# Pooled V from a second read of V, pooled keys as two halves of 72: an attention-then-MLP kernel on one core

## The chip, the core and the metric

The kernel runs on one core of a Trainium2 chip. The time is the device time of one execution in microseconds (us); the median of three runs before the change is 328.3 us (327.95 to 328.8). The core has a matmul engine, TensorE (PE in the profile; its weight loads are listed apart as PEld), three engines for elementwise work (VectorE or DVE, ScalarE or ACT, GpSimd or POOL), a queue engine (SyncE or SP) that issues transfers, and 16 DMA engines that carry them. Data lies in SBUF, 128 partitions wide; matmuls write to PSUM, which GpSimd is not used to read here.

## What is computed

Two parts in a row. Attention over 8 batches, 8 heads, 576 tokens, head size 64, done twice and added:

```python
q_d = q.reshape(B, H, Sd, 4, D).mean(axis=3)      # k_d and v_d in the same way; Sd = 144
out_up = np.repeat(sm_attn(q_d, k_d, v_d), 4, axis=2)
mask = np.abs(pos[:, None] - pos[None, :]) < 4     # local: three tokens to each side
out_local = softmax(where(mask, scale * q @ k.T, -1e9)) @ v
x = (out_up + out_local)  # to rows of 512 = 8 heads x 64, 4608 tokens
h = x @ w_in              # 512 -> 2048
out = (h - tanh(h)) @ w_out   # 2048 -> 512
```

## The kernel before

**Pairs.** Attention goes by pairs of heads: pair p of 32 is batch p // 4, heads 2j and 2j + 1 with j = p % 4. `attention(p)` casts q and k (L452, `qr`), transposes them, from pair 8 on by a DMA transpose (`qT`, L457), puts them in order (`qk`, L465), and pools q and k by sums of four tokens in two additions (`half`, L499; `qkd`, L508). The local scores are five tiles of 128 keys against 112 or 120 queries (`score`, L517). The pooled scores (L539) use `qkd`, whose 144 positions are kept as five overlapping groups of 32, GW = 160 columns, so that pooled positions follow the five tiles of queries; the keys are taken as two overlapping sets of 128. Exponentials are taken on ACT (L557, L569, L572) into `E`, and a 0/1 mask is multiplied in, the big one on DVE (L561), the small one (tile 4, 240 columns, L576) on DVE or GpSimd. Then the values: ten matmuls against `vw` (L585) and eight against the pooled `vd` (L591); a 65th column of ones, or of 0 and 4, gives the sums for the division (L602, L604). The result goes back through a DMA transpose (`lT`, L621) and a `join` of local and pooled parts into `xT` (L633, L637).

**V.** `load_v` brings V as five overlapping tiles of 128 tokens (`vst`, L357), `prep_v` casts it (`vw`, L390). Once for two pairs `pool_v` forms pooled V with TensorE: four matmuls with 32 columns of weights (L405) and one with 128 (L407) into a PSUM bank that the scores or the values use too, copied to `vd` by ACT (L412).

**Dense work.** When a batch's four pairs are in `xT`, `dense` adds its matmuls: `mm1` (L675), tanh on ACT (L686), the difference on DVE (L689), `mm2` (L711), a copy (L726) and the store (L730).

**Order.** `Program` collects all operations with a cost in ns, their reads and writes and a priority, and `order` plays them through engine by engine with these costs; what it gives is the order of instructions of every engine, fixed when the program is built. A `choice` goes to the engine that is free first. Dense matmuls have the last priority, so they fill what attention leaves. SyncE issues in this order: loads of pair p wait, from pair 12 on, until `lT` of pair p - 5 has been issued (`GATE`, `BEHIND`). `SMALL` is the first pair whose small mask may go to GpSimd. Buffers: `vd` and `vw` three, `qk`, `qkd`, `E` two, `vst` five, `qkn` four.

Of the kernel before, what the change touches and what calls it, by code (L numbers as in the profile page):

```python
# [165 lines left out]
def kernel(  # L166
# [21 lines left out]
    NT = 5  # L188
    GS = KW // 4
    PIECES = [(0, 0, 120), (1, 0, 112), (2, 0, 56), (2, 56, 56), (3, 0, 112), (4, 0, 120)]  # L190
    GW = 32 * NT
# [227 lines left out]
    def attention(p):  # L419
# [8 lines left out]
        biased = p < BIASED  # L428

# [72 lines left out]
        def add2(eng):  # L502
            with nc.allow_low_precision("pooled q and k"):
                out = qkd[s].rearrange("p i (t r) -> p i t r", t=NT)
                a, c = (bass.AP(tensor=half.tensor, offset=half.offset + e,
                                ap=[half.ap[0], [2 * G, 2], [2 * GS, NT], [2, 32]])
                        for e in range(2))
                eng.tensor_tensor(out=out, in0=a, in1=c, op=ALU.add)  # L508
# [20 lines left out]
        def s2(bank=ps):  # L529
# [6 lines left out]
            for i in range(2):  # L536
                for hh in range(2):
                    rows = slice(64 * hh, 64 * hh + 64)
                    T.matmul(bank[:, hh, 120 + GW * i:120 + GW * i + GW],  # L539
                             qkd[s][rows, 1, 32 * i:32 * i + 128],  # L540
                             qkd[s][rows, 0], start=True, stop=True)
# [14 lines left out]
        e3 = E[s][:, 1152:1792].rearrange("p (h c) -> p h c", h=2)  # L556
# [9 lines left out]
        if not merged:  # L566
# [6 lines left out]
            out=e3, in_=ps2[:, :, 120:120 + 2 * GW], func=AF.Exp, scale=SCALE / 16.0),  # L573
# [7 lines left out]
        def outs():  # L581
            for hh in range(2):
# [4 lines left out]
                for half in range(2):  # L587
                    c = 1152 + 2 * GW * hh + 128 * half
                    o = 65 * (NT + half)
                    for i in range(2):  # L590
                        T.matmul(po[:, hh, o:o + 65],  # L591
                                 E[s][:, c + GW * i:c + GW * i + 128],
                                 vd[w][:, i, 2 * jj + hh, :],
                                 start=(i == 0), stop=(i == 1))
        if p == 2:
# [3 lines left out]
           reads=[("E", s, 0), ("E", s, 1), ("E", s, 2), ("vw", w, jj), ("vd", w)],  # L599
# [20 lines left out]
        if XOUT[p] == 'dma':  # L620
# [7 lines left out]
            def join(eng):  # L628
# [3 lines left out]
                          for a, n, m in ((x, 456, 120), (pool, 130, 30)))  # L632
# [7 lines left out]
                    in1=pool[:, 32:128].rearrange("p (t g) -> p t g", t=3)[:, :, 2:30]  # L640
# [125 lines left out]
    BYACT = 0  # L766
    T_IN, T_OUT = 1550, 1200
    NOACT = 0
    SMALL = 12
# [131 lines left out]
```

## Time and profile before

| what | value |
|---|---|
| runs, median (lowest to highest) | 328.3 us (327.95 to 328.8) |
| the profiled execution's own time, its span | 327.29 us, 325.6 us |
| granted TensorE clock | 1.0 |
| busy: PE, DVE, ACT, POOL | 313.9, 212.5, 224.7, 165.6 us |
| DMA | 109715 packets, 59.79 MB |
| values of pair 16, 28 and 31 begin (L585, with L602 for the last) | 132.0, 224.6, about 245 us |

Lines beginning with L are groups of instructions: line, engine, operation, output and inputs, shape, count, then busy us and mean ns of one, then the engine's idle time just before them and what ended it. Lines that begin with a number are the timeline: start, length, engine, line, and in brackets the idle time before. "A:B" lines are stretches of the span with the busy time of each engine. Lines with three times and slashes give the minimum, median and maximum of a group in ns. Matmul rows are longer than their slots, since successive matmuls overlap.

### The profile page before, as it was taken

To read this page: it belongs to the slowest core of one execution; us is meant where nothing else is said; L and a number is where in the kernel's file an instruction comes from. 1 tells how busy PE (TensorE), PEld (TensorE's weight loads), DVE (VectorE), ACT (ScalarE), POOL (GpSimd) and SP (SyncE) were. 2 spreads that over 40 slices of the span, in tenths; PEclk is the share of its full clock that TensorE was granted. 3 is DMA by queue.
4 is the path that set the end of the run, shared out by engine and by line. 5 is a ranking of instruction groups with operands and counts; after the bars stand their busy time and mean duration, and the time that the engine had idled before them with its cause. 6 is when DMAs were issued, how large, how long until landed. Compare 5 with 4: busy or idle time off the path is not lost.

```text
span 325.6 us, 7167 instructions
## 1 busy us (share of the span) xinstructions
PE 313.9 (96%) x2643; PEld 175.5 (54%) x2686; DVE 212.5 (65%) x388; ACT 224.7 (69%) x390; POOL 165.6 (51%) x230
## 2 busy tenths in 40 slices
PE   6899999999899999999999999999999999999996
PEld 2565555666544445666654444656554445566544
DVE  6898985789966576765867576778665444554311
ACT  3765987599888969799986978798973444544300
POOL 5688758265846767677767767877440000000000
PEclk9999999999999999999999999999999999999999
DMA  7999999899987999699999999995322001000022
GB/s 205 316 393 367 372 315 273 216 259 217 240 254 106 254 201 294 92 234 219 191 233 165 261 209 263 222 229 106 85 66 62 32 32 67 32 34 32 32 84 81
DMA packets 109715, 59.79 MB, mean 184 GB/s; under 512 B 92656, under 2 KB 92912, under 8 KB 109680
## 3 DMA queue, kind: packets, MB, share of 16 engines
q1 hardware_dynamic: 109680, 59.33, 72.9%
q8 instruction: 21, 0.34, 0.5%
q14 instruction: 14, 0.11, 0.1%
HBM read 37.75 MB, written 9.44 MB: 145 GB/s over the span
## 4 chain that ended last, share of the span: by engine, by line
PE 90%; DVE 4%; issue 2%; POOL 1%; DMA 1%; ACT 1%; SPq 0%; POOLq 0%
PE ps_hy L711 38%; PE ps_hy L675 36%; PE ps_ox L517 3%; PE ps_ox L585 3%; PE ps_ox L591 2%; PE ps_ox L539 1%; PE ps_ox L405 1%; PE ps_ox L618 1%; PE ps_ox L407 1%; DVE ln L604 1%; DVE gT L689 1%; DMA qkn<-in_k_dram 1%; PE ps_ox L615 1%; PE ps_ox L482 1%; PE ps_ts L482 1%
## 5 line engine op out<-in xcount | busy, mean ns | idle before, releaser
L675 PE MATMUL ps_hy<-xT,w_in_sb 128*128 128x320 bf16 (+1 forms) x759 | 146.9, 325 | 1.7 <-DVE gT L689 1.0
L711 PE MATMUL ps_hy<-w_out_sb,gT 128*128 128x512 bf16 (+1 forms) x559 | 139.0, 373 | 2.2 <-issue 1.0
L689 DVE TENSOR_TENSOR gT<-ps_hy,u 128x320 bf16<-128x320 f32 (+1 forms) x192 | 103.2, 553 | 56.0 <-ACT u L686 53.1
L686 ACT ACTIVATE u<-ps_hy 128x320 f32<-128x320 f32 (+1 forms) x192 | 93.6, 497 | 53.2 <-PE ps_hy L675 47.3
L675 PEld LDWEIGHTS <-w_in_sb 128*128 128x128 bf16 x768 | 71.8, 98 | 53.4 <-issue 1.7
L711 PEld LDWEIGHTS <-gT 128*128 128x128 bf16 x592 | 56.0, 98 | 52.8
L499 POOL TENSOR_TENSOR half<-qk 128x576 f32<-128x576 bf16 x29 | 33.3, 1148 | 48.7 <-ACT qk L465 33.9
L465 ACT COPY qk<-qT 128x576 bf16<-128x576 bf16 x44 | 52.3, 1207 | 0.0
L452 POOL CAST qr<-qkn 128x576 bf16<-128x576 f32 x48 | 33.4, 707 | 13.0 <-DMA qkn<-in_k_dram 6.2
L604 DVE TENSOR_TENSOR ln<-ps_ox,r 128x896 bf16<-128x896 f32 x32 | 34.9, 1091 | 1.1
L561 DVE TENSOR_TENSOR E<-E,mask 128x912 bf16<-128x912 bf16 x28 | 24.0, 856 | 10.4 <-ACT E L557 10.4
L557 ACT ACTIVATE E<-ps_ox 128x912 bf16<-128x912 f32 x28 | 26.2, 937 | 4.9 <-PE ps_ox L517 4.6
L726 DVE COPY y<-ps_hy 128x512 f32<-128x512 f32 (+1 forms) x21 | 13.9, 663 | 20.2 <-PE ps_hy L711 19.1
L390 POOL CAST vw<-vst 128x640 bf16<-128x640 f32 x32 | 25.5, 796 | 2.4 <-DMA vst<-in_v_dram 2.3
L508 POOL TENSOR_TENSOR qkd<-half 128x320 bf16<-128x320 f32 x29 | 23.9, 823 | 1.8 <-DVE r L602 1.1
L572 ACT ACTIVATE E<-ps_ox 128x640 bf16<-128x640 f32 x28 | 20.0, 716 | 0.0
L585 PE MATMUL ps_ox<-vw,E 128*128 128x65 bf16 x320 | 19.3, 194 | 0.4 <-ACT vd L412 0.3
L585 PEld LDWEIGHTS <-E 128*128 128x128 bf16 x320 | 16.4, 98 | 5.7 <-issue 0.3
L576 POOL TENSOR_TENSOR E<-E,mask 128x240 bf16<-128x240 bf16 x18 | 13.6, 756 | 9.4 <-ACT E L569 9.3
L591 PE MATMUL ps_ox<-vd,E 128*128 128x65 bf16 x256 | 18.0, 193 | 0.1
L517 PEld LDWEIGHTS <-qk 64*128 64x128 bf16 x320 | 9.2, 95 | 16.1 <-issue 12.5
L602 DVE RECIPROCAL r<-ps_ox 128x14 f32<-128x14 f32 x32 | 7.7, 242 | 14.3 <-PE ps_ox L591 12.4
(78 smaller groups left out, 240.2 us busy)
## 6 DMA issues: line engine op xcount, KB each, us to landing
vst<-in_v_dram SPq DMA_DIRECT2D x64, 160.0 KB, 4.2
qkn<-in_q_dram SPq DMA_DIRECT2D x32, 288.0 KB, 4.1
qkn<-in_k_dram SPq DMA_DIRECT2D x32, 288.0 KB, 4.1
out_dram<-y SPq DMA_DIRECT2D x35, 256.0 KB, 2.5
gT<-in_moe_w_in_dram SPq DMA_DIRECT2D x4, 1024.0 KB, 8.1
xT<-in_moe_w_out_dram SPq DMA_DIRECT2D x8, 256.0 KB, 5.2
gT<-in_moe_w_out_dram SPq DMA_DIRECT2D x2, 1024.0 KB, 10.2
qT<-qr SPq DMA_TRANSPOSE x24, 4.2
```

The lines of the kernel that those rows point to most:

```text
L390: P.choice([(eng, ns, lambda fn=fn: fn(out=vw[w][:, 2 * jj:2 * jj + 2, :, 0:64], in_=vst[s])) for eng, ns, fn in CAST_V[p >= NEARLY]], rea ...
L452: P.choice([(eng, ns, lambda dst=dst, srt=srt, fn=fn: fn(out=dst, in_=srt)) for eng, ns, fn in (any3[2:] if p >= CASTS else any3[:1] + any ...
L465: fn(out=full[:, i].rearrange("p (g a) -> p g a", a=A9), in_=qT[s][:, :, i::2].rearrange("p a g -> p g a"))
L499: eng.tensor_tensor(out=half, in0=four[:, :, :, 0:2], in1=four[:, :, :, 2:4], op=ALU.add)
L557: op("ACT", 820, lambda: A.activation(out=e1, in_=ps[:, :, 0:456], func=AF.Exp, scale=SCALE), reads=ts, writes=[("E", s, 0)], pri=pri)
L585: T.matmul(po[:, hh, 65 * t:65 * t + 65], E[s][:, c:c + 128], vw[w][:, 2 * jj + hh, t, :], start=True, stop=True)
L591: T.matmul(po[:, hh, o:o + 65], E[s][:, c + GW * i:c + GW * i + 128], vd[w][:, i, 2 * jj + hh, :], start=(i == 0), stop=(i == 1))
L604: op("DVE", 1010, lambda: V.tensor_tensor(out=ln[s].rearrange("p n (h d) -> p h n d", d=D), in0=blocks[:, :, :, 0:64], in1=r[s].unsqueeze( ...
L675: T.matmul(ps_hy[slot][:, 0:n], w_in_sb[:, dc, fc * 128:(fc + 1) * 128], xT[dc][:, t0 + c0:t0 + c0 + n], start=(dc == 0), stop=(dc == N_DC ...
L686: op("ACT", 90 + 76 * n // 100, lambda: A.activation(out=u[us][:, 0:n], in_=ps_hy[slot][:, 0:n], func=AF.Tanh), reads=[("hy", slot)], writ ...
L689: op("DVE", 70 + 105 * n // 100, lambda: V.tensor_tensor(out=gT[g][:, fc, c0:c0 + n], in0=ps_hy[slot][:, 0:n], in1=u[us][:, 0:n], op=ALU.s ...
L711: T.matmul(ps_hy[slot][:, 0:c1 - c0], gT[g][:, fc, ts * 128:ts * 128 + 128], w_out_sb[:, fc, c0:c1], start=(fc == 0), stop=(fc == N_FF - 1))
```

## The change

From pair 16 on (`DIRECT`) pooled V no longer comes from `pool_v`, which returns at once. `load_pool` reads V of each head once more, in rows of four tokens: 72 partitions, two rows of 256 numbers on each, into the space of batches 0 and 1 of `xT` (two buffers for each head). These 32 transfers stand in SyncE's queue and, as the other loads, behind the `lT` of five pairs earlier; for pairs 16 and 17 also behind the dense matmuls that read this space. `sum_v` adds the four tokens on GpSimd in two additions for each head and writes `vd` as two sets of 72 keys. For these pairs the pooled positions are plain: `qkd` has 144 columns, the pooled scores are 72 x 144 twice for each head, the exponential takes 72 partitions, and the pooled value matmuls contract 72 rows. `SMALL` becomes 8.

```diff
-    GW = 32 * NT
+    GW, KP = 32 * NT, G // 2
+    def load_pool(p):
+        b, j, n = p // NP, p % NP, p % 2
+        for i in range(2):
+            def issue(i=i, base=v[b, 2 * j + i]):
+                nc.sync.dma_start(out=vp(n, i), in_=bass.AP(
+                    tensor=base.tensor, offset=base.offset,
+                    ap=[[4 * D, KP], [KP * 4 * D, 2], [1, 4 * D]]))
+            load(650, issue, [("vp", n, i)] + [("x", c, 2 * n + i) for c in (0, 1)] * (p < DIRECT + 2),
+                 T_P, -30 + 0.06 + 0.1 * p, behind=[("sent", p - BEHIND)])
+    def vp(n, i):
+        t = xT[2 * n + i][0:KP, 0:1024].bitcast(FP32)
+        return t.rearrange("p (e x) -> p e x", e=2)
+    def sum_v(p):
+        n, w, jj = p % 2, (p // 2) % NVW, p % 2
+        if p < DIRECT + 2 * NVW:
+            op("DVE", 70, lambda: V.memset(vd[w][0:KP, jj, :, 64:65], 4.0),
+               writes=[("vd", w)], pri=10 * p - 12)
+        for i in range(2):
+            t = vp(n, i)
+            def add1(eng, t=t):
+                eng.tensor_tensor(out=t[:, :, 0:128], in0=t[:, :, 0:128],
+                                  in1=t[:, :, 128:256], op=ALU.add)
+            def add2(eng, t=t, i=i):
+                with nc.allow_low_precision("pooled v"):
+                    eng.tensor_tensor(out=vd[w][0:KP, jj, 2 * i:2 * i + 2, 0:64],
+                                      in0=t[:, :, 0:64], in1=t[:, :, 64:128], op=ALU.add)
+            for n1, fn in ((330, add1), (220, add2)):
+                P.choice([("POOL", n1, lambda fn=fn: fn(GP))],
+                         reads=[("vp", n, i)] + [("vd", w)] * (p < DIRECT + 2 * NVW),
+                         writes=[("vp", n, i)] if fn is add1 else [("vdd", w, jj, i)],
+                         pri=10 * p - 8)
     def pool_v(hb):
+        if 2 * hb >= DIRECT:
+            return
     def attention(p):
+        direct = p >= DIRECT
+        gw, kp = (G, KP) if direct else (GW, 128)
         def add2(eng):
+                if direct:
+                    eng.tensor_tensor(out=qkd[s][:, :, 0:G], in0=half[:, :, :, 0],
+                                      in1=half[:, :, :, 1], op=ALU.add)
+                    return
-                    T.matmul(bank[:, hh, 120 + GW * i:120 + GW * i + GW],
-                             qkd[s][rows, 1, 32 * i:32 * i + 128],
-                             qkd[s][rows, 0], start=True, stop=True)
+                    k0 = (KP if direct else 32) * i
+                    T.matmul(bank[0:kp, hh, 120 + gw * i:120 + gw * i + gw],
+                             qkd[s][rows, 1, k0:k0 + kp],
+                             qkd[s][rows, 0, 0:gw], start=True, stop=True)
-            out=e3, in_=ps2[:, :, 120:120 + 2 * GW], func=AF.Exp, scale=SCALE / 16.0),
+            out=e3, in_=ps2[0:kp, :, 120:120 + 2 * gw], func=AF.Exp, scale=SCALE / 16.0),
                         T.matmul(po[:, hh, o:o + 65],
-                                 E[s][:, c + GW * i:c + GW * i + 128],
+                                 E[s][0:kp, c + gw * i:c + gw * i + 128],
+                                 vd[w][0:kp, jj, 2 * hh + i, :] if direct else
                                  vd[w][:, i, 2 * jj + hh, :],
...
+    DIRECT, T_P = 16, 430
-    SMALL = 12
+    SMALL = 8
         if nl[0] < NPAIR:
             load_qk(nl[0])
             load_v(nl[0])
+            if nl[0] >= DIRECT:
+                load_pool(nl[0])
...
         if p + 2 < NPAIR:
             prep_v(p + 2)
+            if p + 2 >= DIRECT:
+                sum_v(p + 2)
```

The `join` reads the pooled part at the plain positions for these pairs; the number and shape of its instructions stay.

More of the change, by code (lines that the diff above doesn't have):

```diff
@@ L555, in attention @@
         e2v = E[s][:, 912:1152].rearrange("p (h c) -> p h c", h=2)
-        e3 = E[s][:, 1152:1792].rearrange("p (h c) -> p h c", h=2)
+        e3 = E[s][0:kp, 1152:1152 + 4 * gw].rearrange("p (h c) -> p h c", h=2)
         op("ACT", 820, lambda: A.activation(
@@ L587, in outs @@
                 for half in range(2):
-                    c = 1152 + 2 * GW * hh + 128 * half
+                    c = 1152 + 2 * gw * hh + 128 * half
                     o = 65 * (NT + half)
@@ L598, in attention @@
         op("PE", 590 * cold, outs,
-           reads=[("E", s, 0), ("E", s, 1), ("E", s, 2), ("vw", w, jj), ("vd", w)],
+           reads=[("E", s, 0), ("E", s, 1), ("E", s, 2), ("vw", w, jj), ("vd", w)] +
+           [("vdd", w, jj, i) for i in range(2)] * direct,
            writes=ox, pri=pri)
@@ L631, in join @@
                                   ap=[a.ap[0], [n, 2], [1, m]])
-                          for a, n, m in ((x, 456, 120), (pool, 130, 30)))
+                          for a, n, m in ((x, 456, 120), (pool, 114 if direct else 130, 30)))
                 eng.tensor_tensor(
@@ L639, in join @@
                     in0=lT[s][:, 1:4, 0:112].rearrange("p t (g a) -> p t g a", a=4),
-                    in1=pool[:, 32:128].rearrange("p (t g) -> p t g", t=3)[:, :, 2:30]
+                    in1=(pool[:, 30:114].rearrange("p (t g) -> p t g", t=3) if direct else
+                         pool[:, 32:128].rearrange("p (t g) -> p t g", t=3)[:, :, 2:30])
                     .unsqueeze(3).to_broadcast([128, 3, 28, 4]), op=ALU.add)
```

## The prediction

> **What bounds the kernel now.** I read the page first, for the engine that sets the end; then the stretches of time; then, inside one stretch, single instructions.
>
> ```profile
> PE 313.9 (96%) x2643; PEld 175.5 (54%) x2686; DVE 212.5 (65%) x388; ACT 224.7 (69%) x390; POOL 165.6 (51%) x230
> ...
> PE 90%; DVE 4%; issue 2%; POOL 1%; DMA 1%; ACT 1%; SPq 0%; POOLq 0%
> ```
>
> TensorE is busy for 96% of the span and is 90% of the chain that ended last. A matmul's row is longer than its slot, so I look at one stretch in the middle: from the value matmuls of pair 16 to those of pair 28.
>
> ```profile
> 132.00:224.60 92.60, 91.50 (x823) 51.96 (x836) 64.84 (x112) 78.58 (x132) 68.49 (x91) 1.00 1.02 213
> 246.00:326.00 80.00, 76.09 (x410) 40.69 (x416) 33.05 (x60) 27.44 (x55) 0.00 (x0) 1.00 0.14 50
> ```
>
> The columns are PE, PEld, DVE, ACT and POOL busy, the granted clock (1.00 throughout), the DMA share and GB/s. In the stretch PE idles 1.1 us in 92.6. GpSimd (POOL) is 74% busy, the DMA engines are occupied without a break (1.02). In the last 80 us GpSimd does nothing and the DMA engines little: what is left is dense work on TensorE. So a microsecond of matmul taken away is a microsecond gained, as long as nothing else makes TensorE wait in the attention stretch; and attention has room to end later, since dense matmuls can be moved ahead of it.
>
> **The matmuls removed.** `pool_v` is skipped eight times, once for every two pairs from pair 16 on; each has 4 matmuls with 32 columns of weights and one with 128.
>
> ```profile
> 137.61 1.03 PE L711 MATMUL ps_hy<-w_out_sb,gT 128*128 128x512 bf16 x4
> 138.56 0.29 PE L405 MATMUL ps_ox<-vw,pick 128*32 128x256 bf16 x4
> 138.79 0.29 PE L407 MATMUL ps_ox<-vw,pick 128*128 128x256 bf16 x1
> 138.91 1.25 PE L675 MATMUL ps_hy<-xT,w_in_sb 128*128 128x320 bf16 x8
> ...
> 140.00 0.32 PE L585 MATMUL ps_ox<-vw,E 128*128 128x65 bf16 x5
> ```
>
> Eight L675 take 1.09 us from start to start, 0.136 each with 320 columns; by columns, 512 take 0.218. The four L711 end their slots at 137.61 + 4 x 0.218 = 138.48, and the next dense matmul starts at 138.91. One `pool_v` costs 0.43 us with its switch between tile shapes. Eight make 3.4 us off TensorE's path.
>
> **Pooled scores, 160 queries become 144.**
>
> ```profile
> 135.41 0.30 PE L539 MATMUL ps_ox<-qkd 64*128 64x160 bf16 x4
> 135.65 1.04 PE L711 MATMUL ps_hy<-w_out_sb,gT 128*128 128x512 bf16 x4
> L539 PEld LDWEIGHTS <-qkd 64*128 64x128 bf16 x128 | 4.8, 94 | 0.0
> L405 PEld LDWEIGHTS <-pick 128*32 128x32 bf16 x64 | 1.6, 92 | 4.6 <-ACT u L686 2.0 <-issue 1.3 <-ACT E L569 0.4
> ```
>
> Four matmuls use 0.24 us; a tenth fewer columns is at most 0.024 us for each of 16 pairs, and I take 0.2 us as the gain after what the switch keeps. Their weights go from 128 columns to 72. No row shows a 72-column load. The nearest rows, 128 and 32 columns, differ by 2 ns, so I take no change; the upper bound is that a narrower load costs its whole slot again, 0.06 us x 64 = 3.8 us. The Trainium skill, "TensorE: Matmul & The Clock Gate", Weight-path perf modes, says that the fast weight load is on only when the number of weights is 128, and its LDWEIGHTS section gives P/1.2 ns for P columns, 60 ns for 72 (estimate): by that rule the 64 loads would take 3.8 us in all, and where they are not covered the gain of the whole change would be about eaten. No run here shows it, and 32 columns would be as quick by that formula as by the row.
>
> The value matmuls keep their number and their 65 columns, but the pooled ones contract 72 rows and not 128.
>
> ```profile
> L618 PE MATMUL ps_ox<-up,ln 32*128 32x120 bf16 x10 | 2.2, 222 | 0.0
> L618 PE MATMUL ps_ox<-up,ln 128*128 128x120 bf16 x10 | 2.2, 217 | 0.0
> ```
>
> With 32 rows a matmul took 222 ns, with 128 rows 217: I take nothing, between -0.6 and +0.6 us (128 x 5 ns).
>
> **ACT and DVE** lose eight pooled-value casts and a tenth of 16 exponentials; DVE gains six memsets. Neither ends TensorE's waits in the stretch: nothing on the path. One small mask more moves to GpSimd in total (pairs 9 and 10 go there, pair 23 comes back): nothing, GpSimd has room before pair 16.
>
> **The additions on GpSimd.** Per pair four instructions are new: two of 256 elements, two of 128, on 72 partitions. The program costs them at 330 and 220 ns when it makes its order. No row has 72 partitions; these have two inputs and 128:
>
> ```profile
> L452 POOL CAST qr<-qkn 128x576 bf16<-128x576 f32 x48 | 33.4, 707 | 13.0 <-DMA qkn<-in_k_dram 6.2 <-DMA qkn<-in_q_dram 2.8 <-DVE ln L604 2.6
> L499 POOL TENSOR_TENSOR half<-qk 128x576 f32<-128x576 bf16 x29 | 33.3, 1148 | 48.7 <-ACT qk L465 33.9 <-ACT qk L486 6.9 <-DVE r L602 4.3
> L390 POOL CAST vw<-vst 128x640 bf16<-128x640 f32 x32 | 25.5, 796 | 2.4 <-DMA vst<-in_v_dram 2.3
> L508 POOL TENSOR_TENSOR qkd<-half 128x320 bf16<-128x320 f32 x29 | 23.9, 823 | 1.8 <-DVE r L602 1.1
> L637 POOL TENSOR_TENSOR xT<-lT 128x336 bf16<-128x336 bf16 x17 | 13.1, 768 | 0.0
> L633 POOL TENSOR_TENSOR xT<-lT x17: 596/600/993, 79.0 to 238.3; 128x240 bf16<-128x240 bf16 x17
> L576 POOL TENSOR_TENSOR E<-E,mask x18: 637/641/1036, 98.1 to 243.3; 128x240 bf16<-128x240 bf16 x18
> ```
>
> From 240 elements (600 ns) to 576 (1148) the slope is 1.63 ns an element, and 336 lies on the line (756 against 768). On it 256 elements cost 0.63 us and 128 cost 0.42: 2.1 us a pair against the 1.1 planned. Lower bound: if time followed partitions, 72/128 of that, 1.2 us, near the plan. Upper bound: each stretched as the longest mask is, 1036/641, 3.4 us. I take 2.1, since its rows are the same operation.
>
> Does that fit? In the changed program's TensorE order 996 dense matmuls stand ahead of pair 31's values where before has 942: attention is spread over more dense work. From pair 16 to pair 28 the added dense columns are worth 9.75 us, and six `pool_v` go: 92.6 + 9.75 - 6 x 0.43 = 99.8 us, if TensorE sets the pace. GpSimd's list between the masks of these pairs has 24 + 24 additions, one more cast of each kind, one more join, one mask fewer, and pooled keys of 288 elements: with the rows' means 71.8 us of old kinds against 70.6. Its occupied 68.5 us become 68.5 + 1.2 + 24 x (1.05 - 0.10 for the overlap of successive instructions) = 92.5, or 93%. That is the narrow place of this change: what is idle now mostly waits for ACT's `qk` (33.9 us in 16 waits in all), and the additions are put into that gap.
>
> What is late behind them is the small mask (L576), which the value matmuls need.
>
> ```profile
> 174.47 1.06 DVE L561 TENSOR_TENSOR E<-E,mask 128x912 bf16<-128x912 bf16 x1
> 174.99 1.04 POOL L576 TENSOR_TENSOR E<-E,mask 128x240 bf16<-128x240 bf16 x1
> 176.68 0.32 PE L585 MATMUL ps_ox<-vw,E 128*128 128x65 bf16 x5
> 184.14 0.64 POOL L576 TENSOR_TENSOR E<-E,mask 128x240 bf16<-128x240 bf16 x1
> 185.19 0.32 PE L585 MATMUL ps_ox<-vw,E 128*128 128x65 bf16 x5
> 189.69 0.79 POOL L576 TENSOR_TENSOR E<-E,mask 128x240 bf16<-128x240 bf16 x1
> 193.26 0.32 PE L585 MATMUL ps_ox<-vw,E 128*128 128x65 bf16 x5
> ```
>
> The mask of pair 22 ended at 176.03 and its values started at 176.68, 0.65 us of slack. The next two pairs have the least and the most of the sixteen, 0.41 and 2.78 us. GpSimd falls 1.0 us a pair behind its plan (2.1 against 1.1), which is more than some of these slacks, and what it still idles, 7.3 us over twelve pairs or 0.6 a pair, takes part of that up. The difference, 0.4 us, would reach TensorE where slack is least; at a quarter of that on average I give back 0.1 us a pair, 1.5 us in all (bounds 0 and rival B).
>
> **The second read of V.** 32 loads more, each of 147 KB in 144 rows of 1 KB, behind the pair's other V loads on SyncE's queue.
>
> ```profile
> q1 hardware_dynamic: 109680, 59.33, 72.9%
> ...
> 132.03 1.29 SPq L457 DMA_TRANSPOSE qT<-qr  x1
> ...
> 203.91 1.24 SPq L621 DMA_TRANSPOSE lT<-ln  x1
> 205.20 1.27 SPq L324 DMA_DIRECT2D qkn<-in_q_dram  x1
> 206.53 0.60 SPq L324 DMA_DIRECT2D qkn<-in_k_dram  x1
> 207.22 0.54 SPq L730 DMA_DIRECT2D out_dram<-y  x1
> 207.82 1.15 SPq L357 DMA_DIRECT2D vst<-in_v_dram  x2
> 209.24 2.18 SPq L457 DMA_TRANSPOSE qT<-qr  x1
> 211.52 1.24 SPq L621 DMA_TRANSPOSE lT<-ln  x1
> ```
>
> By packets a load takes 144/109680, by bytes 0.147/59.33 of 237 us: 0.31 to 0.59 us of all engines, 0.6 to 1.2 us a pair. SyncE's cycle from one `lT` to the next is 7.61 us and nearly full; two issues at 0.58 make 8.8, though 0.89 of the 7.61 is the `qT` issue held back (2.18 against 1.29 after a pause). TensorE's pace is 99.8/12 = 8.3. Loads are gated five pairs ahead, some 41 us, so I cost the second read at nothing on the path; if that cover goes, rival C. The first such load waits until the dense matmuls have read batches 0 and 1 of `xT`, whose space it takes; by its place in SyncE's order that is over.
>
> A load also waits for the additions that last read its buffer, two pairs earlier; behind it on SyncE stand `qT` and `lT` of other pairs, so late additions hold back transposes, and through `lT` the loads five pairs on.
>
> **Sum.** The profiled execution took 327.29 us (span 325.6). 327.29 - 3.4 - 0.2 + 1.5 = 325.2. That execution lies 1.0 us under the median of 328.3, so I forecast 326.2 us.
>
> **Rivals.**
> A is this forecast, own range 324.5 to 327.5.
> D: the additions cost what was planned, because only 72 partitions are used. GpSimd is then 83% occupied (24 x 0.55 = 13.2 us added), nothing is given back: 324.7 us. For it: no row excludes it. Against: the same operation's rows follow elements.
> F: 72-column weight loads are slow. Half of the upper bound, 1.9 us: 328.1 us. For it and against it no row speaks but the two of L539 and L405.
> B, which ends slower: GpSimd becomes the bound from pair 16 on. For it: a mask that overlaps DVE's big mask took 1.04 us, not 0.64; a GpSimd that hardly rests meets every one of DVE's, 0.4 us a pair more, 92.5 + 4.8 = 97.3 of 99.8 us. From there on 2.5 us of waiting in twelve pairs are enough to decide. If a fifth of its present waits for `qk` stays (12 x 2.1 / 5 = 5.1 us), it needs 102.4, 2.6 too many, 3.5 for 16 pairs, on top of the sum: 329.7 us. Against it: the order is made with GpSimd as an engine of its own, and TensorE has later places for pairs. The Trainium skill, "GPSIMD Engine Reference", Specifications, says that GpSimd's SBUF interfaces are shared with VectorE, with contention for DVE instructions with two SBUF inputs; the two rows at 174 agree.
> C: SyncE and the DMA engines. 8.8 us a cycle against 8.3, 0.5 us for each of 16 pairs is 8 us; half of it I take as covered by the five pairs of lead. 326.2 + 4 = 330.2 us. For it: the DMA share of 1.02. Against: in the same stretch TensorE waits 1.1 us in all.
>
> **Chances.** A 0.45, D 0.13, F 0.05, B 0.25, C 0.12. About 0.3% (1 us) is what can be told from no change. Faster: D and nearly all of A, 0.55; the same: F, A's edge and B's mild end, 0.12; slower: 0.33. The range reaches from D without the 1.1 us of waits that the stretch has now, times 16/12, to B and C with half their price again: 323.2 to 331.9.
>
> **What would show it.** Right: L405 has 32 matmuls and not 64; the new additions near 0.63 and 0.42 us; POOL above 90% busy from about 130 to 250 us; PE busy still 98% or more there; attention ending some 9 us later. D shows in additions near 0.33 and 0.22. Wrong: idle time of PE before L585 or L517 released by POOL's mask, `vd` or `qkd` (B), or by transposes and loads that land late, with SyncE's queue held (C). L539 blocks longer than 0.24 us show F.

## The result, and the profile after

The changed kernel takes 1.0055 of the time before, 95% interval 1.0036 to 1.0073: slower by about half a percent, where a faster 326.2 us was forecast. The median over its 22 executions is 330.7 us against 327.8. They lie in two groups, thirteen up to 331.4 us and nine from 333 to 340 us; the ratio leaves the upper group out, as over 1.5% above the fastest, so the median stands beside it. The profiled execution took 335.01 us (span 333.3) and is of the upper group; one of the lower group, on which the ratio rests, is read further below. From the page of the first:

```profile
PE 318.2 (95%) x2646; PEld 176.6 (53%) x2646; DVE 223.2 (67%) x395; ACT 217.8 (65%) x380; POOL 201.3 (60%) x295
PE   6899999999999999996699999999999999999996
PEclk9999999999999999999699999999999999999999
DMA  7999996999999999999377999999942221100012
PE 82%; DVE 5%; issue 5%; ACT 4%; POOL 2%; DMA 1%; SPq 0%; POOLq 0%; ACTq 0%
```

GpSimd has 36 us more work than before. The rows of digits give the busy share, or the clock, in tenths for 40 equal slices of the span. In slices 19 to 22 TensorE, its clock and the DMA engines dip together: one event, not a slow drift. The next fence gives stretches, before and after (columns: PE, PEld, DVE, ACT, POOL busy with counts, granted clock, DMA share, GB/s).

```profile
130.00:250.00 120.00, 118.69 (x1066) 67.88 (x1084) 83.18 (x147) 98.67 (x170) 79.66 (x104) 1.00 0.84 177
```
```profile
130.00:250.00 120.00, 113.14 (x958) 64.70 (x956) 84.34 (x137) 86.95 (x152) 101.64 (x149) 0.97 0.91 208
155.00:161.00 6.00, 0.40 (x3) 0.16 (x2) 6.00 (x2) 0.44 (x1) 5.33 (x9) 0.97 0.59 154
161.00:168.00 7.00, 6.72 (x38) 3.70 (x37) 4.10 (x9) 2.56 (x5) 0.00 (x0) 0.54 0.55 125
168.00:176.00 8.00, 8.00 (x73) 4.59 (x72) 5.61 (x11) 6.17 (x11) 6.86 (x10) 1.00 0.65 194
```

From 130 to 250 us TensorE idles 6.9 us and not 1.3. From 155 to 161 us it does almost nothing, and then it is granted 0.54 of its clock for 7 us, which is worth about 0.46 x 7 = 3.2 us (an estimate). The timeline of the event, engine by engine (start, length, engine, line, and in brackets the idle time before and its releaser), first GpSimd, then VectorE, then TensorE:

```profile
152.62 1.16 POOL L542 TENSOR_TENSOR half<-qk 128x576 f32<-128x576 bf16 x1
153.71 0.67 POOL L495 CAST qr<-qkn 128x576 bf16<-128x576 f32 x1
154.33 0.65 POOL L624 TENSOR_TENSOR E<-E,mask 128x240 bf16<-128x240 bf16 x1
154.93 0.67 POOL L548 TENSOR_TENSOR qkd<-half 128x288 bf16<-128x288 f32 x1
155.54 0.73 POOL L429 CAST vw<-vst 128x640 bf16<-128x640 f32 x1
156.20 0.68 POOL L495 CAST qr<-qkn 128x576 bf16<-128x576 f32 x1
156.83 1.41 POOL L389 TENSOR_TENSOR xT<-xT 72x256 f32<-72x256 f32 x2
158.19 0.87 POOL L394 TENSOR_TENSOR vd<-xT 72x128 bf16<-72x128 f32 x2
159.01 0.60 POOL L683 TENSOR_TENSOR xT<-lT 128x240 bf16<-128x240 bf16 x1
159.56 0.77 POOL L687 TENSOR_TENSOR xT<-lT 128x336 bf16<-128x336 bf16 x1
```
```profile
153.37 7.46 DVE L609 TENSOR_TENSOR E<-E,mask 128x912 bf16<-128x912 bf16 x1 [0.33 <-ACT E L605]
160.75 0.48 DVE L740 TENSOR_TENSOR gT<-ps_hy,u 128x320 bf16<-128x320 f32 x1
```
```profile
154.69 0.71 PE L726 MATMUL ps_hy<-xT,w_in_sb 128*128 128x320 bf16 x4
161.28 1.22 PE L726 MATMUL ps_hy<-xT,w_in_sb 128*128 128x320 bf16 x4 [5.88 <-DVE gT L740]
```

VectorE's big mask (L609, L561 before) takes 7.46 us. Meanwhile GpSimd runs twelve instructions without a pause, each near its shortest length, until 160.33; the mask ends 0.50 us later, a little less than it takes where nothing holds it up (0.62). Behind it on VectorE stands `gT` (L740), for which the dense matmuls wait: 5.88 us. The same mask over the whole program, after and before (count, then minimum, median and maximum in ns), and last what TensorE waited for from 130 to 250 us after the change (in all, times, longest):

```profile
L609 DVE TENSOR_TENSOR E<-E,mask x28: 617/762/7458, 33.5 to 261.5; 128x912 bf16<-128x912 bf16 x28
```
```profile
L561 DVE TENSOR_TENSOR E<-E,mask x28: 615/830/1371, 33.3 to 243.0; 128x912 bf16<-128x912 bf16 x28
```
```profile
PE ps_hy L726 <- DVE gT L740: 6.6, 3, 5.9
PE ps_hy L762 <- DVE gT L740: 0.4, 1, 0.4
```

All of TensorE's waiting in this stretch is behind `gT`; none is behind GpSimd's small mask (L624), `vd` or `qkd`.

### The profile page after: what moved, and what is told of

Same layout as the page of the kernel before. It is cut to its first block, busy times and chain, and to the rows that moved or that the text cites. A ratio compares the mean times of both kernels' runs of the same rounds, so it can differ in the third digit from the quotient of the medians.

```text
span 333.3 us, 7217 instructions
## 1 busy us (share of the span) xinstructions
PE 318.2 (95%) x2646; PEld 176.6 (53%) x2646; DVE 223.2 (67%) x395; ACT 217.8 (65%) x380; POOL 201.3 (60%) x295
## 4 chain that ended last, share of the span: by engine, by line
PE 82%; DVE 5%; issue 5%; ACT 4%; POOL 2%; DMA 1%; SPq 0%; POOLq 0%; ACTq 0%
PE ps_hy L762 35%; PE ps_hy L726 33%; PE ps_ox L633 3%; PE ps_ox L564 3%; PE ps_ox L639 2%; DVE gT L740 1%; ACT qk L508 1%; DVE E L609 1%; DMA qkn<-in_k_dram 1%; PE ps_ox L668 1%; PE ps_ox L587 1%; PE ps_ox L525 1%; PE ps_ox L665 1%; PE ps_ts L525 1%; PE ps_ts L925 1%
## 5 line engine op out<-in xcount | busy, mean ns | idle before, releaser
L726 PE MATMUL ps_hy<-xT,w_in_sb 128*128 128x320 bf16 (+1 forms) x768 | 149.3, 329 | 7.3 <-DVE gT L740 6.8
L762 PE MATMUL ps_hy<-w_out_sb,gT 128*128 128x512 bf16 (+1 forms) x592 | 145.8, 376 | 0.4 <-DVE gT L740 0.4
L740 DVE TENSOR_TENSOR gT<-ps_hy,u 128x320 bf16<-128x320 f32 (+1 forms) x192 | 102.6, 552 | 56.2 <-ACT u L737 53.6
L609 DVE TENSOR_TENSOR E<-E,mask 128x912 bf16<-128x912 bf16 x28 | 30.8, 1100 | 13.4 <-ACT E L605 13.2
L495 POOL CAST qr<-qkn 128x576 bf16<-128x576 f32 x48 | 34.4, 728 | 7.3 <-DMA qkn<-in_k_dram 3.6
L389 POOL TENSOR_TENSOR xT<-xT 72x256 f32<-72x256 f32 x32 | 24.7, 782 | 0.0
L624 POOL TENSOR_TENSOR E<-E,mask 128x240 bf16<-128x240 bf16 x19 | 14.0, 735 | 14.4 <-ACT E L617 13.5
L633 PE MATMUL ps_ox<-vw,E 128*128 128x65 bf16 x320 | 20.0, 196 | 0.3 <-ACT vd L453 0.3
L633 PEld LDWEIGHTS <-E 128*128 128x128 bf16 x320 | 16.8, 99 | 6.2 <-issue 0.3
L620 ACT ACTIVATE E<-ps_ox 72x576 bf16<-72x576 f32 (+1 forms) x28 | 18.9, 676 | 0.0
L639 PE MATMUL ps_ox<-vd,E 128*128 128x65 bf16 (+1 forms) x256 | 18.5, 195 | 0.1
L394 POOL TENSOR_TENSOR vd<-xT 72x128 bf16<-72x128 f32 x32 | 14.8, 471 | 0.9
```

The lines of the kernel that those rows point to most:

```text
L495: P.choice([(eng, ns, lambda dst=dst, srt=srt, fn=fn: fn(out=dst, in_=srt)) for eng, ns, fn in (any3[2:] if p >= CASTS else any3[:1] + any ...
L609: P.choice([(eng, ns, lambda fn=fn: fn(out=e1, in0=e1, in1=mask[:, 0:456].unsqueeze(1).to_broadcast([128, 2, 456]), op=ALU.mult)) for eng, ...
L633: T.matmul(po[:, hh, 65 * t:65 * t + 65], E[s][:, c:c + 128], vw[w][:, 2 * jj + hh, t, :], start=True, stop=True)
L726: T.matmul(ps_hy[slot][:, 0:n], w_in_sb[:, dc, fc * 128:(fc + 1) * 128], xT[dc][:, t0 + c0:t0 + c0 + n], start=(dc == 0), stop=(dc == N_DC ...
L740: op("DVE", 70 + 105 * n // 100, lambda: V.tensor_tensor(out=gT[g][:, fc, c0:c0 + n], in0=ps_hy[slot][:, 0:n], in1=u[us][:, 0:n], op=ALU.s ...
L762: T.matmul(ps_hy[slot][:, 0:c1 - c0], gT[g][:, fc, ts * 128:ts * 128 + 128], w_out_sb[:, fc, c0:c1], start=(fc == 0), stop=(fc == N_FF - 1))
```

## The experiments

**The change again, and its two new kinds of work taken away one at a time.** The first is the changed kernel unaltered. In the second the order is kept, but the additions issue nothing, so the pooled values of the later pairs are not computed. In the third the second read is left out, and the additions work on what lies in the buffer.

```diff
-                P.choice([("POOL", n1, lambda fn=fn: fn(GP))],
+                P.choice([("POOL", n1, lambda: None)],            # second kernel
```
```diff
-                nc.sync.dma_start(out=vp(n, i), in_=bass.AP(...))
+                pass                                              # third kernel
```

> The changed kernel, unaltered, beside the others on one chip. Starvation theory (GpSimd runs instruction after instruction, and the big mask on VectorE, which reads two SBUF tensors, does not get in until GpSimd pauses): 328 to 338 us from run to run, with at least one big mask (L609) above 1.5 us in the trace where before has none above 1.4, and TensorE idle behind it. Transfer theory (the second read of V holds SyncE and the DMA engines): the same times, but TensorE's idle time is released by transposes or loads, and L609 stays near 0.8 us. Lateness theory (GpSimd has too much to do): TensorE's waits are short and spread, before the value matmuls, released by the small mask L624.

> Leaves out the 64 additions on GpSimd (pooled V from pair 16 on is what an earlier pair left in the buffer); the order of all other instructions and the second read stay. Starvation and lateness theories: the removed matmuls show, 327.8 - 3.6 = about 324 us, L609 at most 1.4 us, little scatter. Transfer theory: nothing is gained against the changed kernel, 329 us or more.

> Leaves out the 32 transfers of the second read (the additions work on whatever lies in that space); the order of all other instructions stays. Starvation and lateness theories: no better than the changed kernel, 328 to 338 us, and L609 above 1.5 us at least once, since GpSimd's work is the same. Transfer theory: about 324 us, DMA share in the middle back to before's.

Measured: the change again 1.0037 (1.0002 to 1.0073); without additions 0.9924 (0.9894 to 0.9955), median 325.3 us; without the second read 1.0311 (1.029 to 1.0333). In the repeat a mask took 8.20 us, from 212.70, and TensorE waited 6.99 us; without the read one took 8.21 us and one 4.46. Without additions no mask is above 1.37 us:

```profile
130.00:250.00 120.00, 118.82 (x1029) 68.40 (x1046) 81.17 (x145) 92.47 (x160) 75.59 (x102) 1.00 0.93 211
L609 DVE TENSOR_TENSOR E<-E,mask x28: 623/699/1361, 33.3 to 250.0; 128x912 bf16<-128x912 bf16 x28
```

So the loss is the additions' on GpSimd and not the transfers': the kernel without additions still has the second read, and TensorE idles 1.2 us from 130 to 250 us. The profiled execution shows the whole of what the rest of the change was forecast to be worth: it took 323.49 us, and the forecast's sum without its last term is 327.29 - 3.4 - 0.2 = 323.7. But it is one of the shortest of ten (322.95 to 328.56 us). In the medians the rest is worth 327.5 - 325.3 = 2.2 us and not 3.6; what makes the other executions longer was not traced. Why leaving out the read is worse than the change is open.

**GpSimd made to wait for the big mask.** Before each of its small masks GpSimd copies one element of `E`, which it may do only when the big mask is done.

```diff
+            if eng == "POOL":
+                GP.tensor_copy(out=tick[0:1, 0:1], in_=E[s][0:1, 0:1])
```

> The changed kernel with one element copied by GpSimd out of the exponentials ahead of each small mask that GpSimd does, so that it waits there for the big mask: a pause in which VectorE gets in, at the latest place where it is needed. All orders stay, and GpSimd has 19 instructions of about 0.1 us more. Starvation theory: no L609 above 1.6 us, no standstill of TensorE, 324 to 326 us with little scatter. Lateness theory: slower than the changed kernel by up to 19 x 0.3 = 6 us, since GpSimd loses time. Transfer theory: no change, 329 us or more.

Measured: 1.0175 (1.016 to 1.0191), median 333.1 us, all within 0.9 us. The mask that took 8.20 us near 213 us took 1.18 at its place; others took up to 4.05. GpSimd waited 7.2 us at the copy from 130 to 250 us, and TensorE still idled 6.2 us there, 2.6 of it in one wait for a big mask. The standstills of 5 us and more go, but the starvation theory's expectation failed twice: no mask above 1.6 us, and 324 to 326 us. So this run does not show that the long masks alone make the loss; what GpSimd's own waiting costs was not separated.

**The additions on VectorE, on both, and at their true cost.** The program is planned anew each time.

```diff
-            for n1, fn in ((330, add1), (220, add2)):
-                P.choice([("POOL", n1, lambda fn=fn: fn(GP))],
+                P.choice([("DVE", n1, lambda fn=fn: fn(V))],              # VectorE, 330/220
+            for n1, fn in ((420, add1), (310, add2)):                     # VectorE, 420/310
+            for n1, fn in ((720, add1), (450, add2)):                     # GpSimd, 720/450
+                P.choice([("POOL", 2 * n1 + 50, ...), ("DVE", n1, ...)],  # both
```

> The sixty-four additions are given to VectorE and the order is planned anew; nothing else differs. Starvation theory (VectorE's big mask waits through a whole run of GpSimd instructions that follow without a gap): GpSimd is about as loaded as before the change, near 75% from 132 us on, its runs are short, no big mask is above 2 us, TensorE has no gap of 5 us. VectorE gains 16 x 1.1 us and was 70% busy in that stretch, so it has room: 324.5 to 327.5 us, ratio 0.990 to 0.998. Lateness theory (the additions make the engine that runs them late, because the plan has them too cheap): the same size of loss comes back on VectorE, ratio 1.000 to 1.010, with waits of TensorE behind VectorE's masks and differences but no single instruction above 2 us.

> The additions on VectorE, planned with 420 and 310 ns, the median lengths that they had there, in place of 330 and 220. If the plan's error costs on VectorE too, the ratio falls from 0.9939 by 0.001 to 0.003 (324.6 to 325.4 us); if VectorE has room enough, it stays within 0.001 of 0.9939. No big mask above 2 us in either case.

> The additions stay on GpSimd; only the planner is told 720 and 450 ns for them in place of 330 and 220, near what they take, and makes the order anew. Lateness theory: the loss is the plan's error, and with the true cost the whole saving shows, ratio 0.991 to 0.997. Starvation theory: GpSimd's work is the same and as dense, so big masks above 2 us stay, perhaps at other places; ratio 0.999 to 1.010.

> The kernel planned with 720 and 450 ns once more, for how often its long standstill comes (1 of 9 executions above 333 us before; of the changed kernel 9 of 23). By the starvation theory the other executions, near 326 us, have no big mask above 2 us, and longer executions have one of 5 us or more; ratio of the undisturbed ones 0.994 to 0.998 again.

> Each addition goes to GpSimd (planned at 710 and 490 ns) or to VectorE (330 and 220 ns), whichever the plan has free first, and the order is made anew. Starvation theory: fewer additions on GpSimd, so shorter runs and rarer long masks; between the kernel with all on GpSimd and the one with all on VectorE, ratio 0.990 to 1.004. Lateness theory: the two engines share the work at true cost, nothing is late, ratio 0.990 to 0.996 whether big masks are long or not.

| additions | ratio (interval) | median, us | longest mask of the profile, us |
|---|---|---|---|
| VectorE, 330/220 | 0.9939 (0.9921 to 0.9956) | 325.69 | 1.62 |
| VectorE, 420/310 | 0.9933 (0.9905 to 0.9962) | 325.07 | 1.44 |
| GpSimd, 720/450 | 0.9957 (0.994 to 0.9973) | 326.30 | 10.97, in an execution of 336.0 |
| the same again | 0.9949 (0.9935 to 0.9962) | 326.07 | 2.34 |
| both engines | 1.0094 (1.0066 to 1.0123) | 330.95 | 3.36 |

On VectorE the gain is as large as without additions (0.9924), and this version beats both kernels. There the first addition (L389) takes 0.41 us at best and 0.56 on average, the second (L394) 0.28 and 0.43:

```profile
L389 DVE TENSOR_TENSOR xT<-xT 72x256 f32<-72x256 f32 x32 | 17.2, 555 | 2.0 <-DMA xT<-in_v_dram 1.9
L394 DVE TENSOR_TENSOR vd<-xT 72x128 bf16<-72x128 f32 x32 | 13.6, 431 | 0.2
130.00:250.00 120.00, 119.33 (x1033) 68.16 (x1032) 98.94 (x199) 93.24 (x162) 83.61 (x104) 1.00 0.96 213
```

On GpSimd with true costs most of the gain shows too, which the starvation theory had excluded (0.999 to 1.010 expected): 13 of 14 executions stayed below 327.5 us, where 9 of 22 of the changed kernel took over 333. The fourteenth took 336.0 us, with the longest mask of all; GpSimd's run ends at 197.40 and the mask at 197.88:

```profile
186.91 10.97 DVE L609 TENSOR_TENSOR E<-E,mask 128x912 bf16<-128x912 bf16 x1
...
196.68 0.72 POOL L429 CAST vw<-vst 128x640 bf16<-128x640 f32 x1
```

So the lateness theory is right that the plan matters, and the profiles point to the long masks as the way: the order made with the low costs meets them often, this one seldom. Both engines together missed every expectation, with two masks of 3.3 us and VectorE as full as with all the additions.

**A shorter execution of the changed kernel.**

> The changed kernel once more, unaltered, for a profile of one of its shorter executions (327 to 331.5 us). Starvation theory alone: an execution at 329 us still has big masks of 2 to 4 us, and TensorE's idle time stands behind them. Lateness theory: no big mask above 1.4 us, and TensorE waits 3 to 4 us in all behind small masks, vd or qkd that GpSimd finishes late. In a longer execution (333 us and more) a mask of 5 us or more is expected again by the first.

This one took 329.17 us, a time of the lower group:

```profile
L609 DVE TENSOR_TENSOR E<-E,mask x28: 616/801/4459, 33.4 to 255.7; 128x912 bf16<-128x912 bf16 x28
PE ps_hy L726 <- DVE gT L740: 3.5, 2, 3.0
166.00:172.00 6.00, 6.00 (x59) 3.31 (x58) 3.98 (x9) 4.37 (x7) 3.37 (x6) 1.00 0.85 240
```

The lower group has long masks too. A mask of 4.46 us stopped TensorE for 2.95 us until 165.78, and the clock stays at 1.00 behind that. From 130 to 250 us TensorE idles 120 - 116.05 = 3.9 us, all behind `gT`, against 1.2 without the additions. These 2.8 us are half of the 5.7 between this execution and the 323.49 us; some 1.8 are a clock of 0.91 in the first 20 us, far from these waits, and 1.2 are not assigned. The standstills of 5.88 us above and 6.99 us in the repeat were followed by 0.54 and 0.56 of the clock for 7 us, and both executions are of the upper group. Its nine executions have a mean clock of 0.984 to 0.990, the thirteen others 0.995 and more, so the upper group probably is that of the longest standstills; of the nine only the one above was profiled.

The length of a standstill alone doesn't fix what happens to the clock. In the kernel without the second read TensorE also stood for 2.95 us, until 165.31, and was then granted half:

```profile
165.50:168.90 3.40, 3.40 (x28) 2.13 (x27) 1.73 (x5) 0.44 (x1) 1.45 (x3) 0.50 0.01 4
```

**The mask in 32 bits.** Only the tile that the big mask reads is wider.

```diff
-                out=e1, in0=e1, in1=mask[:, 0:456].unsqueeze(1)...
+                out=e1, in0=e1, in1=wide.unsqueeze(1)...
```

> The order of the changed kernel is kept; only the mask that the big mask multiplication reads is held in 32 bits and not in 16 (one more copy of 456 elements at the start). Starvation theory, narrow form (only VectorE's fast form, two 16-bit inputs from SBUF, needs what GpSimd holds): each big mask takes 1.0 to 1.2 us (estimate from VectorE's own 576-element addition with a 32-bit output, 0.76 us) instead of 0.62, but none above 2 us, and TensorE has no gap of 5 us; VectorE loses about 12 us from 132 us on and has room for most: 325.5 to 329 us, ratio 0.994 to 1.003. Starvation theory, wide form (any VectorE instruction with two inputs from SBUF waits): big masks of 2 to 8 us stay, ratio 1.003 to 1.015.

Measured: 1.0331 (1.0297 to 1.0364). The mask takes 1.09 us at best and up to 4.93, so the long waits are not tied to the 16-bit form. That its longer time makes it meet GpSimd more often, and so costs 3%, is a reading that no run separates.

**The dispute alone.** Four kernels with nothing but GpSimd and VectorE at work.

> A kernel of its own that measures the dispute alone; all of the computation is left out and zeros are stored. In each stretch GpSimd runs 0, 8, 16 or 32 instructions without a gap (the first addition of pooled V, 0.72 us; the cast of q and k, 0.64 us; or both in turn), and VectorE issues four instructions of one form soon after GpSimd's first; six stretches for each of nine combinations. Starvation theory: the first big mask waits until GpSimd's run is over, so its length grows with the run: 0.62 us alone, 4 to 6 us with 8 additions, 9 to 11.5 us with 16, 20 to 23 us with 32, and the other three take 0.62 us; the form with the mask in 32 bits does the same; an instruction with one input in PSUM does not. Rival (one instruction waits for one instruction): each of the four is lengthened by at most one GpSimd instruction, 0.62 to 1.4 us, whatever the length of the run.

> As the first kernel that measures the dispute alone (all of the computation left out, zeros stored), but the GpSimd instructions of a run no longer all depend on the one before: each addition on its own data (free, 8, 16 or 24 of them), on two sets of data in turn (two), every sixth repeating the set before it (some), or all on one set as before (self). Gap theory (VectorE gets in only where GpSimd's next instruction must wait, above all for its own predecessor's result): self as before, 1.0 us a mask; free: the first mask waits until the run ends, 5 to 6 us with 8, 10.5 to 11.5 us with 16, 16 to 17 us with 24, the others 0.62; some: 3 to 4.5 us and then more; the 32-bit mask as the free ones, the instruction with an input in PSUM 0.69 us. Rival (a GpSimd instruction always lets VectorE in at its end, and the long waits of the kernel have another cause): 1.0 us a mask in every stretch.

> A third kernel that measures the dispute alone (computation left out, zeros stored), with GpSimd's own instructions of the attention stretch in place of one addition: ten stretches each of half, qkd, small masks, the two casts, the join and the second addition, and of the whole list of a pair twice over (22 instructions, as they stand at 153 us of the changed kernel); VectorE's big mask starts at another phase in each stretch, three times in the long ones. Form theory (some of these instructions, one after another, do not let VectorE in between): in the list some masks take 3 to 15 us, ending 0.5 us after GpSimd's last, and one or more of the single kinds give masks as long as the kind's whole run (2.5 to 5 us). Rival (it needs more than GpSimd and VectorE: transfers, ACT or TensorE at work beside them): every mask at 0.62 to 1.5 us here too.

> A fourth kernel that measures the dispute alone (computation left out, zeros stored): in each stretch GpSimd runs 8 to 22 independent instructions of one kind, of two or three kinds in turn, or a pair's whole list twice, and VectorE puts four big masks along it, the later ones further into the run than in the first two such kernels. Two readings of the list's masks of 2.1 to 3.8 us: place in the run (GpSimd lets VectorE in during its first instructions only, since it has not yet fetched ahead): then the third and fourth mask take 3 us and more in every kind, single kinds too, and self-dependent additions alone stay near 1.0 us. Sequence (small mask, qkd, cast of V let VectorE in at none of their ends, other sequences do): long masks, 2 us and more, only where small, qkd and the cast follow one another (three, smallqkd, qkdvw, list), and single kinds stay below 1.5 us.

```diff
+        for r in range(6):
+            ...                                  # GpSimd waits for VectorE's last
+            for i in range(n):
+                g(i)                             # a run of n GpSimd instructions
+            d_mask(e)                            # VectorE, beside them
```

First and second: the mask takes 0.63 us alone and 0.63 to 1.06 us beside additions or casts, dependent or not, in runs of 8 to 32. One GpSimd instruction ends, the mask runs, and the next GpSimd instruction is longer by about 0.4 us. Both the starvation theory and, in the second, the gap theory (that a dependence decides) gave this wrong. An instruction with an input in PSUM took 0.63 to 0.69 us beside GpSimd. Third: the list of a pair, as GpSimd has it in the kernel, brings the long masks back, with no transfer, ACT or TensorE at work:

```profile
355.41 1.14 POOL L71 TENSOR_TENSOR halfb<-qkb 128x576 f32<-128x576 bf16 x1
356.50 0.66 POOL L88 CAST qrc<-qkna 128x576 bf16<-128x576 f32 x1
357.12 0.63 POOL L79 TENSOR_TENSOR Fb<-Fb,mask 128x240 bf16<-128x240 bf16 x1
357.72 0.66 POOL L75 TENSOR_TENSOR qkdb<-halfb 128x288 bf16<-128x288 f32 x1
358.32 0.72 POOL L84 CAST vwb<-vstb 128x640 bf16<-128x640 f32 x1
358.98 1.07 POOL L88 CAST qrd<-qknb 128x576 bf16<-128x576 f32 x1
```
```profile
355.73 3.80 DVE L104 TENSOR_TENSOR E_list<-E_list,mask 128x912 bf16<-128x912 bf16 x1
...
372.10 3.70 DVE L104 TENSOR_TENSOR E_list<-E_list,mask 128x912 bf16<-128x912 bf16 x1
```

Four ends of GpSimd instructions pass before the fifth lets VectorE in, seen in the lengthened 1.07 us. In the next stretch the mask starts later in the run and takes 0.10 us less: the same end lets it in. But the place in the list alone doesn't fix that end: behind `half`, the first that was passed here, VectorE got in when its mask had begun one instruction earlier, in a later stretch (1.97 us, from 468.54). Fourth: every single kind and every alternation of two or three, masks placed late in the run, stayed at 1.37 us or less; only the list gave more.

```profile
L104 DVE TENSOR_TENSOR E_self<-E_self,mask x24: 620/834/1095, 25.0 to 97.5; 128x912 bf16<-128x912 bf16 x24
L104 DVE TENSOR_TENSOR E_three<-E_three,mask x24: 622/823/1197, 801.3 to 876.7; 128x912 bf16<-128x912 bf16 x24
L104 DVE TENSOR_TENSOR E_list<-E_list,mask x24: 623/1082/3778, 880.7 to 971.3; 128x912 bf16<-128x912 bf16 x24
```

So neither the place in the run nor the sequence small mask, `qkd`, cast explains it, and none of these kernels reached the 7 to 11 us of the whole one. What decides which ends let VectorE in stays open.

**Dependence between GpSimd's instructions, in the kernel.** In the first a one-element copy of its own result follows each first addition, the order being kept; in the others both additions of a head are one unit, planned at 550 or 1200 ns.

```diff
+                eng.tensor_copy(out=tick[0:1, 0:1], in_=t[0:1, 0, 0:1])   # first
...
+            P.choice([("POOL", 550, both)],                               # second; 1200 in the third
```

> The order of the changed kernel is kept, and all its work; behind each first addition GpSimd copies one element of the result, so that it must wait for its own predecessor (32 more instructions, 0.18 us each, some 6 us more for GpSimd). Gap theory: a mask never waits past the next pair's additions, so none above 5 us is left (7.5 to 11 us before), and executions above 336 us go; median 327 to 331 us, ratio 0.999 to 1.010, in spite of the added work. Lateness theory: GpSimd is 6 us later in sixteen pairs, the median rises to 332 to 336 us.

> The two additions of a head are planned and issued as one unit of 550 ns (330 and 220 as before), so that each second addition waits for the first just before it; no work is added. Gap theory: GpSimd lets VectorE in twice a pair, no mask above 5 us, executions above 336 us go, ratio 0.997 to 1.004 with a median below the changed kernel's 330.7. Lateness theory: the same work at the same planned cost, ratio 1.002 to 1.010 and long executions as often as before (about 4 in 10).

> The same unit, planned at 1200 ns (measured 0.72 and 0.46). Gap and lateness theory together: no mask above 5 us, no execution above 330 us, ratio 0.993 to 0.997, as the kernel planned with 720 and 450 in its undisturbed executions (0.9957 and 0.9949), whose one long execution had a mask of 10.97 us.

Measured: 1.0462 (1.044 to 1.0484), 1.0082 (1.0059 to 1.0105) and 1.0086 (1.0051 to 1.012). The first has masks of up to 6.10 us, the others of 4.16 and 3.51; not only the mask is held up, VectorE's `join`, also of two SBUF inputs, took up to 3.30 us in the first and 3.11 in the second; TensorE's waits behind `gT` are 10.1, 3.3 and 3.8 us from 130 to 250 us, and 1.1 and 1.2 us behind the small mask in the units. The gap theory fails here too, and 1200 ns for the unit lost what 720 and 450 had gained, so a cost near the truth is no remedy by itself. Over the profiles of all these kernels the order by longest mask is not exactly the order by time, but none with a mask above 2.4 us is faster than before, and all that are faster in their profile stay at 2.34 us or below.

## Why the prediction was wrong

**Right: the matmuls removed.** `pool_v` falls from 64 to 32 matmuls of L405 (now L446). Without additions the values of pairs 16 and 28 (L633) begin at 130.25 and 229.95 us, 99.7 us apart, where the prediction has 99.8, and the profiled execution took 323.49 us against 323.7; in the medians, as said, 2.2 of the 3.6 us show. Right too: 72-column weights cost TensorE nothing that shows, so rival F falls. Four pooled score matmuls (L587) use 151.05 - 150.83 = 0.22 us, against 0.24 before, and 0.22 in all sixteen pairs. By the Trainium skill, "TensorE: Matmul & The Clock Gate", Weight-path perf modes, the fast weight load is on when the number of weights is 128. The rows of the 72-column loads are indeed longer, 110 ns against 94, but that stays covered:

```profile
150.83 0.29 PE L587 MATMUL ps_ox<-qkd 64*72 64x144 bf16 x4
151.05 0.99 PE L726 MATMUL ps_hy<-xT,w_in_sb 128*128 128x320 bf16 x6
L587 PEld LDWEIGHTS <-qkd 64*72 64x72 bf16 x64 | 2.7, 110 | 0.0
```

**Right: the second read is hidden.** With it, and without the additions, TensorE idles 1.2 us from 130 to 250 us, as before; without it the kernel was not faster. Rival C falls.

**A size off: the additions.** Estimated 0.63 and 0.42 us; the means are 0.78 and 0.47 us, with undisturbed ones at 0.72 and 0.45, so 2.5 us a pair and not 2.1. No saving by fewer partitions shows; rival D falls.

```profile
L389 POOL TENSOR_TENSOR xT<-xT 72x256 f32<-72x256 f32 x32 | 24.7, 782 | 0.0
L394 POOL TENSOR_TENSOR vd<-xT 72x128 bf16<-72x128 f32 x32 | 14.8, 471 | 0.9
```

**Wrong: the step that gave back 1.5 us.** It took GpSimd's lateness at the small mask as the only way in which the additions reach TensorE, and put VectorE at nothing on the path. How full GpSimd gets was forecast well, 92.5 of 99.8 us between the values of pairs 16 and 28; in the execution of 329.17 us it is 94.2 of 104.3:

```profile
131.10:235.40 104.30, 100.35 (x865) 57.43 (x864) 74.61 (x123) 79.17 (x138) 94.16 (x139) 1.00 1.03 228
```

But the loss doesn't come from there: from 130 to 250 us TensorE waits for `gT`, behind VectorE's big mask, in the profiled execution of 335.01 us and in that of 329.17 us, and never for the small one. With kernels run side by side the additions cost 8.4 us in the medians (333.7 for the repeat, 325.3 without them) and 3.7 us by the ratios (1.0037 and 0.9924); 1.5 us was forecast. The account of the first profiled execution: 323.7, plus 6.9 - 1.3 = 5.6 us more idle from 130 to 250 us, plus 3.2 us of lower clock, is 332.5 of the 335.0 us measured; the other 2.5 us are not assigned. Two of the prediction's signs of being right failed with this step: from 130 to 250 us TensorE was 94% busy and not 98, and GpSimd 85% and not above 90, in the execution of 335.01 us.

**Rival B had the right pair of engines and the wrong victim.** It took the row at 174 us, a small mask of 1.04 us beside a big one, as a price of 0.4 us that GpSimd pays for each meeting. The mirror case, VectorE paying for a whole run of GpSimd, was not considered; the trace of before, with 1.37 us as the longest mask, doesn't show it. Its time, 329.7 us, lies near the measured one by luck: with GpSimd at 101.6 of 120 us it is not the bound. It is luck too that the median lies inside the forecast's range, whose upper part stands on B and C. The Trainium skill, "GPSIMD Engine Reference", Specifications, names the contention, with VectorE instructions of two SBUF inputs, that the runs show. That one instruction can wait through a whole run of others is what these traces add.

## What to carry to other kernels

When work is moved to GpSimd beside a VectorE that multiplies two SBUF inputs, look not only at GpSimd's share but at the longest single VectorE instruction before and after: a share of 60% over the span was enough for waits of ten times the instruction's length. The same additions on VectorE, which had the room, kept the gain (0.9933). Telling the planner the measured cost of each addition kept more than half of it on GpSimd (0.9957 and 0.9949), though with a rare long standstill, while 1200 ns for two of them as a unit did not (1.0086). So a planner's error of 1.4 us a pair (2.5 against 1.1) seems to have mattered less through the work itself than through which neighbours the order made meet; that is a reading of these runs, not shown by one of them.

## What the hardware showed unexpectedly

A VectorE multiplication of 0.62 us waited 7.5, 8.2 and 11.0 us through ten and more successive GpSimd instructions, which ran near their shortest lengths, and ended about 0.5 us after the last. With one kind of GpSimd instruction, or two or three in turn, it never waited for more than the one in progress (1.37 us at most); with a pair's list it waited up to 3.80 us with nothing else running. And after standstills of 5.9 and 7.0 us TensorE was granted 0.54 and 0.56 of its clock for 7 us. After shorter ones it went either way: after 2.95 us the full clock in one execution and half of it for 3.4 us in another, after 2.58 us (the unit planned at 550 ns) half of it, after 3.76 us (the kernel with the one-element copies of its own result) the full clock.
